# Softmax row sums: addition and reciprocal on GpSimd in place of VectorE

## The chip, the cores and the metric

The kernel runs on one core of a Trainium2 chip. A core has five engines with instruction queues of their own, each working through its queue in order: TensorE (PE, with its weight loads shown as PEld), VectorE (DVE), ScalarE (ACT), GpSimd (POOL) and SyncE (SP), which here issues the DMAs. They work at the same time and wait for one another by semaphores. The metric is the time of one execution on the device in microseconds, the median of several.

## What is computed

Attention with a learned bias of relative position, and after it a soft mixture of experts over the tokens of all eight batches. The part that matters here is the softmax of the attention:

```
scores = scale * q @ k^T + bias
scores = scores - max(scores, axis=-1)
attn = exp(scores)
attn = attn / (sum(attn, axis=-1) + 1e-09)
out  = attn @ v
```

There are 8 batches and 8 heads, 576 positions and a head width of 64, all in 32-bit floats. The mixture of experts then has 32 slots over 512 features, and takes the softmax of its logits once over the tokens and once over the slots. The change touches neither of these two softmaxes, only that of the attention.

## The kernel before

The kernel first builds the table of the bias (some 36 jobs, steps f, B, E, D), stores it in HBM, and reads it back for each pair of heads. Then come 32 units, each a pair of heads of one batch. A unit is cut into row blocks of 128 query positions: four for every unit, and for every second unit a fifth, which holds the last 64 positions of two units. That makes 144 row blocks. Each row block goes through these steps, with p the block and u the unit:

- S (L439, L444): PE multiplies queries and keys, 288 columns at a time, for two heads.
- t (L459): VectorE adds the bias to the scores in PSUM, writes the result to a tile y of 2 x 576 columns in SBUF, and keeps the running minimum (the sign is turned) in mn. Four instructions a block.
- e (L468): ScalarE takes the exponential of 576 columns in place, and puts their sum into one of the two columns of the tile sm. Two instructions a block.
- m (L475, L476): VectorE adds 1e-9 to both columns of sm and takes the reciprocal. This is the step that changes.
- n (L374, called at L483): GpSimd multiplies 576 columns of y by one column of sm, in place. Two instructions a block.
- T and R (L423): PE turns the block through its transposes into PSUM; c and cR (L377): VectorE or ScalarE, as the order says, copies it to the tiles at and ar.
- M and Mr (L547, L557): PE multiplies with the values; x (L377) copies the result to xts.

The last pair of heads adds the steps of the mixture of experts for each batch (L582 to L841), and after the loop come the experts' matrices and the output (L967 to L1075).

The order of all these steps is written out by hand in the string ORDER (L23 on). Each step has one place in it, such as `m0/5` for step m of block 0 in unit 5. The program issues the steps sorted by their place, so every engine gets its own instructions in that order, and none overtakes another on the same engine. The buffers are rotated: four tiles y, four tiles mn and four tiles sm. A tile of sm is written by e, worked on by m and read by n. All DMAs of the loop are issued by SP.

Before the loop, a small tile nb1 (L309) holds the negative of a bias column, one column wide; VectorE reads it at L902 while the table of the bias is built. GpSimd has a few tasks of its own at the start (the identity matrix, zeroing, rsum, the sign of phi at L301), and during the loop only step n and seven small memsets (L690).

Of the kernel before, what the change touches and what calls it, by code (L numbers as in the profile page):

```python
# [10 lines left out]
F32 = mybir.dt.float32  # L11
F32R = mybir.dt.float32r
AF = mybir.ActivationFunctionType
ALU = mybir.AluOpType
# [214 lines left out]
def body(ctx, tc, qk, v, wcol, phi, mw1, mw2, tabh, consth, out, outr):  # L229
    nc = tc.nc  # L230
    P = 128
# [8 lines left out]
    const = ctx.enter_context(tc.tile_pool(name="const", bufs=1))  # L240
# [46 lines left out]
    cols = const.tile([P, 2 + H], F32, name="cols")  # L287
# [18 lines left out]
            nc.gpsimd.memset(t, 0.0)  # L306

    last = {}
    nb1 = const.tile([P, 1], F32, name="nb1")  # L309
    nc.vector.tensor_scalar(out=nb1, in0=cols[:, 1:2], scalar1=-1.0, scalar2=None, op0=ALU.mult)  # L310
    wbd = const.tile([P, 32], F32, name="wbd")
    nc.vector.memset(wbd, 0.0)
    for g in range(4):
        rs = slice(32 * g, 32 * g + 32)
        nc.vector.tensor_scalar(out=wbd[rs, H * g:H * g + H], in0=cols[rs, 2:2 + H], scalar1=1.0 / QS, scalar2=None,
                                op0=ALU.mult)
# [108 lines left out]
    def rows(u, p):  # L425
# [46 lines left out]

        def sums(_):
            r = d["sm", p]
            nc.vector.tensor_scalar(out=r, in0=r, scalar1=1e-9, scalar2=None, op0=ALU.add)  # L475
            nc.vector.reciprocal(out=r, in_=r)  # L476

        step(u, f"m{p}", sums)
        for g in range(2):

# [683 lines left out]
```

## Time and profile before

| | |
|---|---|
| median of three executions | 583.1 us (582.52 to 585.4) |
| span of the profiled execution | 579.5 us (its time as a whole is not shown) |
| VectorE, addition at L475 | 144 instructions, 251 ns in the mean |
| VectorE, reciprocal at L476 | 144 instructions, 166 ns in the mean |
| GpSimd, scaling at L374 | 288 instructions, 746 ns in the mean |
| ScalarE, exponential at L468 | 288 instructions, 770 ns in the mean |

The span runs from the first to the last instruction that the profiler saw; a whole execution is a little longer. In the profile's rows, `y<-y,sm` names the tile that is written and those that are read, `128x2 f32` is partitions by elements, and `x144` is the number of instructions. Busy time comes first, then the mean of one instruction, then the idle time of the engine just before them with what ended it. A wait with several causes is put down to the last one by the profile. "The chain" is the work that ended last, followed back from the last instruction; "the loop" here is the window from 60 to 500 us.

### The profile page before, as it was taken

The numbers are of one execution on the slowest core, as the hardware profiler recorded it, in microseconds if no ns is written. First come the engines' busy times: TensorE is split into PE (matmuls) and PEld (weight loads), VectorE is DVE, ScalarE is ACT, GpSimd is POOL, SyncE is SP. The second block draws the span as 40 slices with busy tenths as digits, with TensorE's granted clock in tenths as the row PEclk, the third lists the DMA queues.
The fourth block names the chain that finished last, engine by engine and source line by source line (L and its number), as shares of the span: only waits on it lengthen the run. The fifth ranks groups of instructions, "written<-read, shape, count | busy, mean of one in ns | idle before, by whom it ended". The sixth has DMA issues, their size and how long they took to land.

```text
span 579.5 us, 19040 instructions
## 1 busy us (share of the span) xinstructions
PE 546.3 (94%) x7235; PEld 351.7 (61%) x7235; DVE 452.6 (78%) x1808; ACT 460.0 (79%) x959; POOL 217.6 (38%) x308
## 2 busy tenths in 40 slices
PE   5989899999999999999999999999999999979992
PEld 3445566666766666666776666676666666643541
DVE  7998878788889788888788888888997889761322
ACT  6989889988888998888988889888879788431332
POOL 4000545555545454454544454545235331400000
PEclk9999899999999999999999999999999999999997
DMA  5698523164865154777522266430533534799968
GB/s 157 225 321 292 167 64 111 56 195 136 293 188 190 51 176 154 255 240 248 170 82 83 85 202 185 148 117 29 184 138 124 173 128 155 260 401 409 403 273 314
DMA packets 43869, 109.89 MB, mean 190 GB/s; under 512 B 8449, under 2 KB 8577, under 8 KB 43777
## 3 DMA queue, kind: packets, MB, share of 16 engines
q1 hardware_dynamic: 43776, 108.67, 54.5%
q8 instruction: 57, 0.93, 0.7%
q14 instruction: 36, 0.29, 0.2%
HBM read 81.25 MB, written 27.41 MB: 188 GB/s over the span
## 4 chain that ended last, share of the span: by engine, by line
PE 64%; DVE 11%; ACT 10%; DMA 6%; issue 4%; POOL 2%; SPq 0%; ACTq 0%; POOLq 0%; DVEq 0%
PE ps L547 16%; PE ps L439 16%; PE ps L423 13%; DVE y L459 6%; ACT y L468 4%; PE ps L444 3%; PE ps L557 3%; PE ps L1030 2%; POOL y L374 2%; PE ps L986 2%; ACT f L900 2%; PE ps L911 2%; ACT e L921 2%; DMA bias_m<-e 1%; DMA xo<-xs 1%
## 5 line engine op out<-in xcount | busy, mean ns | idle before, releaser
L374 POOL TENSOR_SCALAR y<-y,sm 128x576 f32<-128x576 f32 x288 | 210.4, 746 | 274.0 <-DVE sm L476 213.8
L468 ACT ACTIVATE y<-y,mn 128x576 f32<-128x576 f32 x288 | 220.8, 770 | 20.3 <-DVE mn L459 15.5
L439 PE MATMUL ps<-qk 64*128 64x288 f32 x1024 | 160.2, 422 | 1.2 <-DMA qk<-in_qk_dram 0.4
L377 ACT COPY at<-ps 128x1024 f32<-128x1024 f32 (+2 forms) x151 | 132.1, 895 | 23.2 <-PE ps L423 19.3
L547 PE MATMUL ps<-at,v 128*64 128x320 f32 (+1 forms) x1024 | 133.7, 410 | 0.7 <-DMA v<-in_v_dram 0.4
L459 DVE CUSTOM_DVE_ANT_0 y<-ps,bm,mn 128x288 f32<-128x288 f32 x256 | 123.5, 512 | 8.8 <-PE ps L439 3.4
L423 PEld LDWEIGHTS ps<-ident,y 64*128 64x128 f32 x2592 | 100.0, 139 | 43.4 <-POOL y L374 17.8
L459 DVE CUSTOM_DVE_ANT_0 y<-ps,bm 128x288 f32<-128x288 f32 x256 | 108.3, 453 | 15.0 <-PE ps L439 8.7
L423 PE MATMUL ps<-ident,y 64*128 64x64 f32 x2592 | 113.3, 227 | 3.4 <-DVE mn L459 1.0
L439 PEld LDWEIGHTS ps<-qk 64*128 64x128 f32 x1024 | 100.3, 187 | 18.7 <-DVE mn L459 2.8
L547 PEld LDWEIGHTS ps<-at,v 128*64 128x64 f32 x1024 | 70.4, 137 | 54.6 <-DVE mn L459 6.9
L468 ACT ACTIVATION_READ_ACCUMULATOR y<-y,mn 128x1 f32 x288 | 54.9, 191 | 0.0
L475 DVE TENSOR_SCALAR sm<-sm 128x2 f32<-128x2 f32 x144 | 36.1, 251 | 20.4 <-ACT y L468 20.0
L911 PE MATMUL ps<-f,wbd 128*32 128x79 f32 (+45 forms) x640 | 43.4, 407 | 7.0 <-DVE f L902 4.2
L902 DVE TENSOR_SCALAR f<-tabs,scl,nb 128x560 f32<-128x560 f32 (+17 forms) x106 | 45.8, 506 | 2.7 <-DMA tabs<-in_tab_dram 0.9
L459 DVE DVE_READ_ACCUMULATOR2_ANT mn<- 128x1 f32 x576 | 47.6, 83 | 0.0
L911 PEld LDWEIGHTS ps<-f,wbd 128*32 128x32 f32 x640 | 22.8, 114 | 27.9 <-issue 10.1
L377 DVE COPY at<-ps 128x1024 f32<-128x1024 f32 (+2 forms) x41 | 31.2, 763 | 5.5 <-PE ps L423 5.0
L900 ACT ACTIVATE f<-tabs,cols,scl 128x432 f32<-128x432 f32 (+15 forms) x38 | 26.5, 753 | 2.5 <-DMA bias_m<-e 2.5
L476 DVE RECIPROCAL sm<-sm 128x2 f32<-128x2 f32 x144 | 23.8, 166 | 4.9
L921 ACT ACTIVATE e<-ps,bcon 128x591 f32<-128x591 f32 x36 | 25.8, 769 | 0.3 <-PE ps L911 0.3
L444 PE MATMUL ps<-qk 64*64 64x288 f32 x256 | 22.6, 429 | 1.5 <-ACT at L377 1.2
(151 smaller groups left out, 430.5 us busy)
## 6 DMA issues: line engine op xcount, KB each, us to landing
wt<-in_moe_w_dram SPq DMA_DIRECT2D x62, 512.0 KB, 7.1
qk<-in_qk_dram SPq DMA_DIRECT2D x32, 576.0 KB, 4.1
bias_m<-e SPq DMA_DIRECT2D x32, 295.5 KB, 3.4
v<-in_v_dram SPq DMA_DIRECT2D x32, 288.0 KB, 4.4
out_dram<-ob SPq DMA_DIRECT2D x16, 512.0 KB, 5.7
xs<-xts SPq DMA_DIRECT2D x24, 288.0 KB, 3.7
xo<-xs SPq DMA_DIRECT2D x8, 864.0 KB, 4.9
bm<-bias_m SPq DMA_DIRECT2D x16, 288.0 KB, 4.1
```

The lines of the kernel that those rows point to most:

```text
L374: nc.gpsimd.tensor_scalar(out=out, in0=y, scalar1=r, scalar2=1.0, op0=ALU.mult, op1=ALU.mult)
L377: (nc.vector.tensor_copy if eng else nc.scalar.copy)(out=out, in_=in_)
L423: nc.tensor.matmul(out, src[rs], ident[rs, rs], is_transpose=True, start=True, stop=True, tile_position=(64 * r, 0))
L439: nc.tensor.matmul(pss[hh].t[:, 0:HALF], x[rs, S + p * P:S + (p + 1) * P], x[rs, k0:k0 + HALF], start=True, stop=True, tile_position=(64 * ...
L444: nc.tensor.matmul(pss[hh].t[64 * r:64 * r + 64, 0:HALF], x[rs, S + 512:2 * S], x[rs, k0:k0 + HALF], start=True, stop=True, tile_position= ...
L459: nc.vector.tensor_tensor_reduce(out=d["y", p][:, hs], in0=d["ps", p, n][hh].read()[:, 0:HALF], in1=biases[hp][p][:, hs], scale=-QS, scala ...
L468: nc.scalar.activation(out=y, in_=y, func=AF.Exp, bias=d["mn", p][:, 2 + hh:3 + hh], scale=-1.0, accum_out=d["sm", p][:, hh:hh + 1])
L547: nc.tensor.matmul(po.t[o:o + 64, 0:wide[c]], d["v"][:, 64 * (4 * hh + i):64 * (4 * hh + i) + 64], main[:, :, 4 * hh + i, :], start=i == 0 ...
L900: nc.scalar.activation(out=f, in_=tabs[:, 0:n], func=AF.Relu, bias=cols[:, 1:2], scale=sc)
L902: nc.vector.tensor_scalar(out=f, in0=tabs[:, 0:n], scalar1=sc, scalar2=nb1[:, 0:1], op0=ALU.mult, op1=ALU.max)
L911: nc.tensor.matmul(pb.t[32 * t:32 * t + 32, a // 512, a % 512:a % 512 + c1 - c0], wbd, x, start=True, stop=True, tile_position=(0, 32 * t))
L921: nc.scalar.activation(out=e, in_=x, func=AF.Identity, bias=bcon[:, k:k + 1])
```

## The change

Both instructions of step m go to GpSimd. The addition becomes a tensor_scalar with two operations, an addition of 1e-9 and a multiplication by 1. The reciprocal becomes a tensor_tensor that raises sm to the power of a second tile, which holds -1 in both columns. That tile is part of nb1, now four columns wide, and is set by a memset of GpSimd at the start; VectorE writes only the first column of nb1 now. Step m keeps its places in ORDER, and nothing else is changed.

```diff
-    nb1 = const.tile([P, 1], F32, name="nb1")
-    nc.vector.tensor_scalar(out=nb1, in0=cols[:, 1:2], scalar1=-1.0, scalar2=None, op0=ALU.mult)
+    nb1 = const.tile([P, 4], F32, name="nb1")
+    minus = nb1[:, 2:4]
+    nc.gpsimd.memset(minus, -1.0)
+    nc.vector.tensor_scalar(out=nb1[:, 0:1], in0=cols[:, 1:2], scalar1=-1.0, scalar2=None, op0=ALU.mult)
...
         def sums(_):
             r = d["sm", p]
-            nc.vector.tensor_scalar(out=r, in0=r, scalar1=1e-9, scalar2=None, op0=ALU.add)
-            nc.vector.reciprocal(out=r, in_=r)
+            nc.gpsimd.tensor_scalar(out=r, in0=r, scalar1=1e-9, scalar2=1.0, op0=ALU.add, op1=ALU.mult)
+            nc.gpsimd.tensor_tensor(out=r, in0=r, in1=minus, op=ALU.pow)
```

## The prediction

> **What bounds the kernel now.** I read the page's first parts, then the table of engine times for the loop alone, then the chain and the waits. The page gives the frame:
>
> ```profile
> span 579.5 us, 19040 instructions
> ...
> PE 546.3 (94%) x7235; PEld 351.7 (61%) x7235; DVE 452.6 (78%) x1808; ACT 460.0 (79%) x959; POOL 217.6 (38%) x308
> ...
> PE 64%; DVE 11%; ACT 10%; DMA 6%; issue 4%; POOL 2%; SPq 0%; ACTq 0%; POOLq 0%; DVEq 0%
> ```
>
> The edit acts in the attention loop only, about 60 to 500 us. The table of busy times for that window (us busy, instructions in brackets):
>
> ```profile
> core 0: us, PE busy (x) PEld busy (x) DVE busy (x) ACT busy (x) POOL busy (x), PEclk, DMA share, GB/s
> 60.00:500.00 440.00, 432.70 (x5687) 291.36 (x5688) 370.19 (x1596) 383.79 (x826) 209.55 (x293) 1.00 0.46 151
> ```
>
> TensorE is busy 432.7 of 440 us at a granted clock of 1.00, so only 7.3 us are plainly idle there. A busy PE is not quite a full one, though. On the chain, the same eight score products take two lengths (start, us, what):
>
> ```profile
> 69.84 1.24 PE ps L439 x8
> ...
> 79.14 1.02 PE ps L439 x8
> ```
>
> 1.02 us when they run back to back, 1.24 when something is waited for in between. So PE is the bound, with a few us of slack inside it; VectorE (84% of the loop) and ScalarE (87%) are close behind, GpSimd (48%) is not. What can be gained is limited by PE, and what can be lost is not limited at all. The groups the edit touches, in the page's list of costliest groups:
>
> ```profile
> L374 POOL TENSOR_SCALAR y<-y,sm 128x576 f32<-128x576 f32 x288 | 210.4, 746 | 274.0 <-DVE sm L476 213.8
> ...
> L475 DVE TENSOR_SCALAR sm<-sm 128x2 f32<-128x2 f32 x144 | 36.1, 251 | 20.4 <-ACT y L468 20.0
> ...
> L476 DVE RECIPROCAL sm<-sm 128x2 f32<-128x2 f32 x144 | 23.8, 166 | 4.9
> ```
>
> There are 144 row blocks, each with one addition, one reciprocal and two scalings by GpSimd.
>
> **What is removed.** VectorE loses 36.1 + 23.8 = 59.9 us of work, and 20.4 + 4.9 = 25.3 us in which it stood still in front of these two. That is 85 us of its 440. Only the part on the chain can shorten the kernel. In the chain of work, followed through the loop in pieces of 40 us, L475 and L476 stand in 39 rows with 7.1 us together; the first two and the last two are:
>
> ```profile
> 100.95 0.09 DVE sm L475
> 101.06 0.18 DVE sm L476
> ...
> 480.03 0.18 DVE sm L475
> 480.23 0.04 DVE sm L476
> ```
>
> They come in two kinds. Six times, first at 100.95 and last at 444.48 us, the chain goes on from the reciprocal to GpSimd's scaling (0.27 + 0.53 + 0.54 + 0.75 + 0.86 + 0.27 = 3.2 us of the 7.1). The other times, 3.9 us, it goes on to VectorE's next score addition at L459, which merely stood behind them in VectorE's queue. The second kind vanishes.
>
> Part of that time is waiting inside the instruction. The instructions of the two lines, minimum, median and maximum in ns:
>
> ```profile
> L475 DVE TENSOR_SCALAR sm<-sm x144: 147/168/749, 58.1 to 497.7; 128x2 f32<-128x2 f32 x144
> L476 DVE RECIPROCAL sm<-sm x144: 165/166/168, 58.3 to 498.0; 128x2 f32<-128x2 f32 x144
> ```
>
> The addition has a median of 168 and a maximum of 749, about one scaling of GpSimd (746); the reciprocal never varies. So the addition is sometimes held while GpSimd works on SBUF: (251 - 168) x 144 = 12 us, within the 36.1, which goes too.
>
> **What is added.** GpSimd gets 144 additions and 144 powers on 128x2, and one memset at the start (I cost it at nothing: GpSimd stands 7.2 us for the phi load at the start, the first row below, and a 128x1 memset takes 0.1 us, the last row, which is the price without that cover). No row shows a power, nor a 128x2 operation of GpSimd. The nearest, in the list of groups on that engine:
>
> ```profile
> L301 POOL TENSOR_SCALAR phis<-phis 128x256 f32<-128x256 f32 x1 | 3.7, 3737 | 7.2 <-DMA phis<-in_moe_phi_dram 7.2
> ...
> L303 POOL TENSOR_TENSOR rsum<-rsum,ident 128x32 f32<-128x32 f32 x1 | 0.2, 249 | 0.0
> ...
> L1141 POOL MEMSET const-float32-1.0<- 128x1 f32 x1 | 0.1, 98 | 0.0
> ```
>
> Each is bounded below by 0.1 us (the memset) and above by 3.7 us (the dearest single instruction of this engine, though on 256 columns and beside VectorE's run of f additions). For the addition I take 0.25 us, the two-operand row, which has sixteen times the columns. For the power I take 0.25 us too, since two columns can hold little beyond the fixed cost; this is the weakest number here, and its upper end makes the second rival. Together 0.5 us a block, 72 us in all: GpSimd goes from 209.6 to about 281 of 440 us, still the least loaded engine.
>
> On this place the Trainium skill speaks against the change: "GPSIMD Engine Reference", section "Engine selection", sends elementwise work to VectorE and puts GpSimd at about half its speed for two inputs. By it the pair would take about 2 x (251 + 166) = 0.83 us, an estimate, and the gain below would be about 3 us smaller; no row here shows the pair.
>
> **The path of one block.** From the end of the exponential's sum to the scaling, in the timeline at 217 us:
>
> ```profile
> 217.54 0.19 ACT L468 ACTIVATION_READ_ACCUMULATOR y<-y,mn 128x1 f32 x1
> ...
> 217.75 0.17 DVE L475 TENSOR_SCALAR sm<-sm 128x2 f32<-128x2 f32 x1 [0.93 <-ACT y L468]
> 217.96 0.17 DVE L476 RECIPROCAL sm<-sm 128x2 f32<-128x2 f32 x1
> ...
> 218.29 2.90 POOL L374 TENSOR_SCALAR y<-y,sm 128x576 f32<-128x576 f32 x4 [0.90 <-DVE sm L476]
> ```
>
> 217.73 to 218.29: 0.56 us when VectorE was already waiting. After the change: 0.5 us of work and a hop less. So the unobstructed path stays about as long; what goes is VectorE's queue ahead of it.
>
> **The added wait.** GpSimd now waits for the exponential itself. Queued behind it are the block's own two scalings and, by a count in the written ORDER, in 43 of the 144 blocks also scalings of another block, ahead of the block's own; those could pass before, and now stand behind an exponential. PE's turns (T, R) wait for the scalings, and through the four y buffers the later score additions. No DMA is moved: all go by SP, which has neither step.
>
> ```profile
> POOL y L374 <- DVE sm L476: 213.8, 80, 44.3
> ...
> DVE sm L475 <- ACT y L468: 20.0, 33, 1.8
> ...
> PEld ps L423 <- POOL y L374: 17.8, 42, 0.6
> ...
> DVE y L459 <- PE ps L439: 12.1, 21, 1.2
> ```
>
> In this list of waits (us, times, longest) PE's weight loads stood 42 times for a scaling, 0.42 us each, and another view has the matmuls themselves idle for it for 0.8 us in four waits: mostly the wait hides under matmuls that are still running.
>
> ```profile
> PE ps L423 <- POOL y L374: 0.8, 4, 0.3
> ```
>
> **The sum.** On the chain 7.1 us go. Back come 6 x 0.5 = 3.0 us where the chain went through the pair to GpSimd, and at most 4 x 0.5 = 2.0 us for the four visits to GpSimd that had no pair in front. That leaves 2.1 us at the worst, 7.1 at the best. I take 3.6: nearer the low end, because behind each gap PE's own order is late next. Span 579.5 - 3.6 = 575.9. The executions' median is 583.1, 3.6 us above the profiled span (start and end around it; the profiled execution's own total is not shown), so 583.1 - 3.6 = **579.5 us**, its own range 576 to 582.
>
> **Rivals.**
>
> *No gain.* PE is busy for 98% of the loop, so what VectorE leaves turns into VectorE waiting for PE (already 12.1 us at L459, in the list of waits), and the in-order waits on GpSimd eat the rest. About 583, within 2.
>
> For it speaks PE's 432.7 of 440; against it the chain, which leaves PE for VectorE and ScalarE for 21% of the span. Another reason for the same outcome would be that VectorE's remaining work is held by GpSimd's longer activity:
>
> ```profile
> L459 DVE CUSTOM_DVE_ANT_0 y<-ps,bm,mn x256: 495/514/519, 47.6 to 493.0; 128x288 f32<-128x288 f32 x128
> ```
>
> L459 is 495 to 519 ns at every one of 256, with GpSimd busy nearly half the time, so it is never held. The Trainium skill, "Perfetto Trace Analysis", section "Optimizing Scalar/DVE Operations", warns that the two engines share an SBUF port, so that offloading between them might not help. By that warning the time would be 583; this row bears it out for L475 only, the instruction that leaves.
>
> *A dear power: slower.* If the pair takes 1.5 us instead of 0.5, the scalings come 1.5 - 0.56 = 0.94 us later. Where PE waited already, 42 times, some 0.42 us hide as they do now, so 42 x 0.52 = 22 us are lost: about 605. The loss begins near 0.56 + 0.42 = 1.0 us a pair. From (440 - 209.6) / 143 = 1.6 us GpSimd itself is the bound; at 3.7 us for the power alone it would need 144 x (1.49 + 0.25 + 3.7) = 783 us for a loop of 440, a time above 900. Against it: two columns, the 249 ns row. For it: a power is not an addition or a product, and none of this engine's rows does more than these.
>
> *The change doesn't do what it says.* The steps could keep VectorE waiting through another dependence, for instance on the shared tile nb1. VectorE writes nb1 once and waits there for a DMA anyway; nothing follows. It would give 583 and is counted with no gain.
>
> **How the numbers follow.** Forecast (pair up to 0.7 us, gain 1 to 10): 0.48, of which 0.40 beyond 0.5% and 0.08 within. No gain: 0.22, all within 0.5%. Dear power: 0.30, of which 0.28 slower beyond 0.5% and 0.02 within; a third of it, 0.10, lies above 605. About 0.5% (2.9 us) is what a measurement of this kernel tells from no change; the three runs of before span that. So faster 0.40, same 0.32, slower 0.28. The range goes down to 573, where the 7.3 idle us of PE and an estimated 3 us of stretched products are gone, and up to 605, the dear power at 1.5 us; above and below lie about 0.15.
>
> **What would show it.** Right: GpSimd's two new groups at 0.2 to 0.35 us each, its busy time in the loop near 281 us; VectorE near 310 us, with L459 waiting longer for PE; no VectorE row of sm; L374 still near 746 ns. PE's weight loads wait for L374 no more than 18 us. Wrong in price: a power above 0.7 us, GpSimd above 340 us, PE idle for L374 for several us. Wrong in the order: GpSimd idle for exponentials while scalings lie behind, and PE's turns waiting for those.

## The result: slower by 9%, and the profile after

The changed kernel took 635.75 us (632.7 to 641.02), the kernel before 582.81 beside it: ratio 1.0912, 95% interval 1.0855 to 1.097. The forecast was 579.5 with a range of 573 to 605, so the sign was wrong and the time lies outside the range. Ratios compare undisturbed executions alone: one of the nine of the kernel without any pair, below, took 1299.89 us and does not enter its ratio. (Lines of the changed kernel are two higher behind the edit: the pair is L477 and L478, the scaling L376, the score addition L461, the turns L425.)

The page of the changed kernel, span and busy times:

```profile
span 630.9 us, 19013 instructions
...
PE 554.6 (88%) x7235; PEld 345.5 (55%) x7235; DVE 404.7 (64%) x1520; ACT 461.7 (73%) x959; POOL 346.2 (55%) x597
```

VectorE lost 452.6 - 404.7 = 48 us of busy time. The prediction took off 59.9, the two groups' times added up; but their records overlap in time with those of VectorE's neighbouring instructions, and without the pair the busy time of before would be 406.9 us, 46 less. GpSimd gained 346.2 - 217.6 = 129 us instead of 72. The loop now ends near 550 us. The list of groups on GpSimd shows the price of each step:

```profile
L376 POOL TENSOR_SCALAR y<-y,sm 128x576 f32<-128x576 f32 x288 | 210.9, 747 | 8.6
L478 POOL TENSOR_TENSOR sm<-sm,nb 128x2 f32<-128x2 f32 x144 | 100.7, 699 | 12.0
L477 POOL TENSOR_SCALAR sm<-sm 128x2 f32<-128x2 f32 x144 | 27.6, 192 | 177.5 <-ACT y L470 170.4
```

The addition takes 192 ns, the scaling is unchanged, and the power takes 699 ns on two columns. One block in GpSimd's timeline shows the gaps as well (start, us):

```profile
240.06 0.19 POOL L477 TENSOR_SCALAR sm<-sm 128x2 f32<-128x2 f32 x1
240.34 0.70 POOL L478 TENSOR_TENSOR sm<-sm,nb 128x2 f32<-128x2 f32 x1
241.13 1.47 POOL L376 TENSOR_SCALAR y<-y,sm 128x576 f32<-128x576 f32 x2
```

From the start of the addition to the scaling are 1.07 us: 0.89 of work and two gaps of 0.09. The path before was 0.56 us. No wait is printed at 240.06: GpSimd came to this pair late, straight from other scalings. The list of waits (total, times, longest) shows where the time went:

```profile
POOL sm L477 <- ACT y L470: 170.4, 59, 42.9
PEld ps L425 <- POOL y L376: 78.4, 93, 2.4
ACT at L379 <- PE ps L425: 61.0, 66, 2.7
PE ps L425 <- POOL y L376: 48.9, 69, 2.3
```

PE itself now stands idle 69 times for a scaling, 48.9 us, where it was 0.8 us in four. That is nearly the whole loss, 53 us of time and 51 us of the profiled span. Only 59 of the 144 pairs begin with a wait for the exponential; 84 of the others start within 0.1 us of the end of GpSimd's earlier work, so there GpSimd is already behind. ScalarE's copies wait for the late turns in their turn. The chain of work is no use here: its printed shares add up to about half the span, so I don't read it.

### The profile page after: what moved, and what is told of

Read it like the earlier page. It is cut to its first block, busy times and chain, and to the rows that moved or that the text cites. A ratio compares the mean times of both kernels' runs of the same rounds, so it can differ in the third digit from the quotient of the medians.

```text
span 630.9 us, 19013 instructions
## 1 busy us (share of the span) xinstructions
PE 554.6 (88%) x7235; PEld 345.5 (55%) x7235; DVE 404.7 (64%) x1520; ACT 461.7 (73%) x959; POOL 346.2 (55%) x597
## 4 chain that ended last, share of the span: by engine, by line
PE 20%; POOL 17%; ACT 6%; DVE 4%; issue 3%; DMA 1%; POOLq 0%; DVEq 0%; SPq 0%; ACTq 0%
POOL y L376 11%; POOL sm L478 5%; PE ps L425 4%; ACT y L470 4%; PE ps L441 3%; PE ps L1032 2%; PE ps L988 2%; DVE y L461 2%; PE ps L549 2%; DMA xo<-xs 1%; POOL sm L477 1%; PE ps L1065 1%; ACT at L379 1%; PE ps L765 1%; DVE ob L379 1%
## 5 line engine op out<-in xcount | busy, mean ns | idle before, releaser
L376 POOL TENSOR_SCALAR y<-y,sm 128x576 f32<-128x576 f32 x288 | 210.9, 747 | 8.6
L425 PE MATMUL ps<-ident,y 64*128 64x64 f32 x2592 | 118.5, 229 | 50.4 <-POOL y L376 48.9
L441 PE MATMUL ps<-qk 64*128 64x288 f32 x1024 | 157.3, 425 | 0.4 <-DVE ck L741 0.3
L425 PEld LDWEIGHTS ps<-ident,y 64*128 64x128 f32 x2592 | 98.5, 140 | 102.6 <-POOL y L376 78.4
L461 DVE CUSTOM_DVE_ANT_0 y<-ps,bm 128x288 f32<-128x288 f32 x256 | 108.2, 454 | 42.4 <-PE ps L441 26.3
L461 DVE CUSTOM_DVE_ANT_0 y<-ps,bm,mn 128x288 f32<-128x288 f32 x256 | 123.1, 514 | 16.4 <-PE ps L441 8.2
L477 POOL TENSOR_SCALAR sm<-sm 128x2 f32<-128x2 f32 x144 | 27.6, 192 | 177.5 <-ACT y L470 170.4
L478 POOL TENSOR_TENSOR sm<-sm,nb 128x2 f32<-128x2 f32 x144 | 100.7, 699 | 12.0
L441 PEld LDWEIGHTS ps<-qk 64*128 64x128 f32 x1024 | 94.4, 190 | 20.7 <-DVE mn L461 3.0
L461 DVE DVE_READ_ACCUMULATOR2_ANT mn<- 128x1 f32 x576 | 47.8, 83 | 0.0
L379 DVE COPY ar<-ps 128x256 f32<-128x256 f32 x22 | 9.3, 424 | 33.9 <-PE ps L425 33.8
L379 DVE COPY xts<-ps 128x320 f32<-128x320 f32 (+1 forms) x26 | 11.4, 455 | 26.8 <-PE ps L559 25.3
```

What stands on the lines that cost most here:

```text
L376: nc.gpsimd.tensor_scalar(out=out, in0=y, scalar1=r, scalar2=1.0, op0=ALU.mult, op1=ALU.mult)
L379: (nc.vector.tensor_copy if eng else nc.scalar.copy)(out=out, in_=in_)
L425: nc.tensor.matmul(out, src[rs], ident[rs, rs], is_transpose=True, start=True, stop=True, tile_position=(64 * r, 0))
L441: nc.tensor.matmul(pss[hh].t[:, 0:HALF], x[rs, S + p * P:S + (p + 1) * P], x[rs, k0:k0 + HALF], start=True, stop=True, tile_position=(64 * ...
L461: nc.vector.tensor_tensor_reduce(out=d["y", p][:, hs], in0=d["ps", p, n][hh].read()[:, 0:HALF], in1=biases[hp][p][:, hs], scale=-QS, scala ...
L477: nc.gpsimd.tensor_scalar(out=r, in0=r, scalar1=1e-9, scalar2=1.0, op0=ALU.add, op1=ALU.mult)
```

## The experiments

Two theories. **Price**: the pair's length on GpSimd makes the scalings late, and PE waits for them. **Order**: GpSimd's place in the order is at fault, since ready scalings stand behind its wait for another block's exponential.

### Length of the pair

A product in place of the power:

```diff
-    nc.gpsimd.memset(minus, -1.0)
+    nc.gpsimd.memset(minus, 0.001)
...
-            nc.gpsimd.tensor_tensor(out=r, in0=r, in1=minus, op=ALU.pow)
+            nc.gpsimd.tensor_tensor(out=r, in0=r, in1=minus, op=ALU.mult)
```

> The power becomes a product with a constant 0.001, in the same place; the reciprocal is left out, so the attention is scaled wrongly, and only the time counts. Price theory (the long power, 0.70 us, makes the scalings late): the pair shrinks from 1.07 us to about 0.55 us per block, as long as VectorE's pair was, and the time goes back to 578 to 590. Order theory (GpSimd waits in its queue for an exponential, and ready scalings of other blocks stand behind it): the waits stay, 610 to 636.

Measured 589.36 us, ratio 1.0117 (1.008 to 1.0155). Its group and PE's wait:

```profile
L478 POOL TENSOR_TENSOR sm<-sm,nb 128x2 f32<-128x2 f32 x144 | 28.1, 195 | 12.0
```

```profile
PE ps L425 <- POOL y L376: 11.9, 27, 1.2
```

A product has 195 ns where the power has 699, the pair is 0.56 us, and most of the loss is gone. So the power's half microsecond is the main cause. But the 0.56 us on GpSimd are not free either.

Three additions in place of one:

```diff
             nc.gpsimd.tensor_scalar(out=r, in0=r, scalar1=1e-9, scalar2=1.0, op0=ALU.add, op1=ALU.mult)
+            nc.gpsimd.tensor_scalar(out=r, in0=r, scalar1=1e-9, scalar2=1.0, op0=ALU.add, op1=ALU.mult)
+            nc.gpsimd.tensor_scalar(out=r, in0=r, scalar1=1e-9, scalar2=1.0, op0=ALU.add, op1=ALU.mult)
             nc.gpsimd.tensor_tensor(out=r, in0=r, in1=minus, op=ALU.pow)
```

> The changed kernel with the addition made three times, two more instructions of 0.19 us with their gaps, 0.55 us more per block. Price theory: as much again as the power's 0.5 us cost, 680 to 700 (144 x 0.37 us more). Order theory: the waits for the exponential are no longer, 636 to 650.

Measured 710.22 us, 1.2198 (1.2142 to 1.2255), above even the price theory's range. PE's idle time for the scalings:

```profile
PE ps L425 <- POOL y L376: 96.9, 87, 3.9
```

The power alone:

```diff
-            nc.gpsimd.tensor_scalar(out=r, in0=r, scalar1=1e-9, scalar2=1.0, op0=ALU.add, op1=ALU.mult)
             nc.gpsimd.tensor_tensor(out=r, in0=r, in1=minus, op=ALU.pow)
```

> The changed kernel without the addition of 1e-9 (left out): the power alone, 0.70 us and a gap, 0.79 us per block in place of 1.07. Price theory: between the runs with a pair of 0.55 us (589.4) and of 1.07 us (635.8), by the line through them 605 to 616. If the power's presence counted, and not the length: 630 to 636.

Measured 600.13 us, 1.0254 (1.02 to 1.0309), below the straight line. Taking 0.28 us from the pair gives back 36 us.

And the zero of the curve, no pair on any engine:

```diff
-            nc.vector.tensor_scalar(out=r, in0=r, scalar1=1e-9, scalar2=None, op0=ALU.add)
-            nc.vector.reciprocal(out=r, in_=r)
+            pass
```

> The kernel before with neither addition nor reciprocal on any engine (both left out; the scaling multiplies by the sum itself, so the attention is not normalised). The whole of VectorE's relief, with nothing given back: the zero of the curve of the pair's length. By the forecast's chain at most 7.1 us go, so 576 or more. If the relief is worth more than the chain shows, as the run without the addition (576.3 with half of it) suggests: 566 to 574.

Measured 578.44 us, 0.9918 (0.9885 to 0.9951), a gain of 4.8 us: within the 7.1 of the forecast's chain, and not the 566 to 574 of the other reading.

| pair on GpSimd, start to scaling | time | ratio to before | PE idle for the scalings |
|---|---|---|---|
| none | 578.4 us | 0.992 | none listed |
| 0.56 us (product) | 589.4 | 1.012 | 11.9 us, 27 times |
| 0.79 (power alone) | 600.1 | 1.025 | 19.2, 37 |
| 1.07 (the change) | 635.8 | 1.091 | 48.9, 69 |
| 1.63 (three additions) | 710.2 | 1.220 | 96.9, 87 |

The slope is 20 us of time for a microsecond of pair up to 0.56, then 47, and 127 to 133 beyond 0.79. The runs come from different sets; by the ratios the steps are 21, 35, and 134 to 137. With 144 blocks, the last figure means that about 0.9 of every microsecond added to a block arrives at the end. Not all of that is waiting. With the longest pair the granted clock of the profiled execution is 0.942, where the changed kernel has 0.987; a score product (L441) takes 460 ns instead of 425, and PE is busy 29 us longer. PE's idle time for the scalings grew by 48 of the 73 us by which the span grew. Why the clock was lower is open.

### Place in the order

The pair directly ahead of the block's own first scaling (`done` is an empty set at the start):

```diff
-        step(u, f"m{p}", sums)
...
             def scale(_, g=g):
+                if (u, p) not in done:
+                    done.add((u, p))
+                    sums(0)
                 y = d["y", p][:, S * g:S * g + S]
```

> The changed kernel with the pair moved in GpSimd's queue to directly ahead of the block's own first scaling, so that no other block's scaling stands behind its wait. Order theory: most of the 53 us come back, 583 to 600. Price theory: pair and price are as before, 620 to 640.

Measured 633.17 us, 1.087 (1.0817 to 1.0922), against 635.75. The same edit on the product version:

> The product version (589.4) with the pair moved directly ahead of the block's own first scaling; the reciprocal is left out. Order theory for what was left there: 581 to 585. Price theory (0.55 us of occupation for each block): 587 to 592.

Measured 586.08 us, 1.0046 (1.0028 to 1.0064), against 589.36, between the two ranges. Both moves give back about 3 us, the first within the intervals, the second just beyond them. The order theory is worth that and no more.

The wait by itself was tried twice. The first form reads the sums on GpSimd ahead of VectorE's pair (`spare` is a further part of nb1, kept for no use):

```diff
+            nc.gpsimd.tensor_scalar(out=spare, in0=r, scalar1=1e-9, scalar2=1.0, op0=ALU.add, op1=ALU.mult)
             nc.vector.tensor_scalar(out=r, in0=r, scalar1=1e-9, scalar2=None, op0=ALU.add)
             nc.vector.reciprocal(out=r, in_=r)
```

> The kernel before, with VectorE's pair as it was, and on GpSimd, in the place of the pair, one addition of 0.19 us that reads the sums and writes a spare tile: the wait in GpSimd's queue without the price. Order theory: most of the 6.7 us that the product version still lost, 588 to 595. Price theory: 583 to 587, 0.28 us of occupation.

Measured 608.74 us, 1.0398 (1.0335 to 1.0462): too much for either theory. The list of waits names a wait that I had built in myself:

```profile
DVE sm L479 <- POOL nb L478: 70.3, 84, 2.3
```

VectorE works on sm in place, so it may not begin before GpSimd has read it, and stood 70.3 us for that. The clean form lets VectorE write two columns of mn that are free by then:

```diff
+            nc.gpsimd.tensor_scalar(out=spare, in0=r, scalar1=1e-9, scalar2=1.0, op0=ALU.add, op1=ALU.mult)
-            nc.vector.tensor_scalar(out=r, in0=r, scalar1=1e-9, scalar2=None, op0=ALU.add)
-            nc.vector.reciprocal(out=r, in_=r)
+            nc.vector.tensor_scalar(out=d["mn", p][:, 0:2], in0=r, scalar1=1e-9, scalar2=None, op0=ALU.add)
+            nc.vector.reciprocal(out=d["mn", p][:, 0:2], in_=d["mn", p][:, 0:2])
...
-                norm(y, y, d["sm", p][:, g:g + 1])
+                norm(y, y, d["mn", p][:, g:g + 1])
```

> The kernel before, VectorE's pair writing its result to two spare columns of mn, and on GpSimd in the pair's place one addition of 0.19 us that reads the sums and writes a spare tile. As the run with the wait alone (608.7), but VectorE no longer waits for GpSimd to have read the sums. If that wait of VectorE made the 608.7: 584 to 592. If GpSimd's own wait in its queue did: 600 to 610.

Measured 590.87 us, 1.0127 (1.0098 to 1.0155). Its control has the same addition on constants, behind the block's second scaling:

```diff
-            nc.gpsimd.tensor_scalar(out=spare, in0=r, scalar1=1e-9, scalar2=1.0, op0=ALU.add, op1=ALU.mult)
...
                 norm(y, y, d["mn", p][:, g:g + 1])
+                if (u, p) in done:
+                    nc.gpsimd.tensor_scalar(out=spare, in0=minus, scalar1=1e-9, scalar2=1.0, op0=ALU.add, op1=ALU.mult)
+                done.add((u, p))
```

> The same kernel with GpSimd's addition on constants behind the block's second scaling, with no wait: its occupation alone. Price theory: 583 to 590 and within 3 us of the run with the clean wait. Order theory: that run is at least 8 us slower than this one.

Measured 588.88 us, 1.0102 (1.007 to 1.0134). The wait is worth 2 us, within the intervals nothing. But 0.19 us of GpSimd per block, which nobody waits for, already cost 6 us. PE's idle time for the scalings is 5.3 us in that run, where it was 0.8 before. Both runs also write VectorE's result to mn, and that was not timed by itself.

### The path, or GpSimd's occupation

One power per block behind the second scaling, nothing in the path:

```diff
                 norm(y, y, d["sm", p][:, g:g + 1])
+                if (u, p) in done:
+                    nc.gpsimd.tensor_tensor(out=spare, in0=minus, in1=minus, op=ALU.pow)
+                done.add((u, p))
```

> The kernel before, with VectorE's pair as it was, and one power per block on a spare tile, on GpSimd behind the block's second scaling: GpSimd's extra occupation without a longer path in the block itself and without a wait. If occupation is what costs: 600 to 620. If only the path from exponential to scaling costs, or the order: 583 to 588.

Measured 600.6 us, 1.0299 (1.0256 to 1.0342). Occupation alone costs 18 us, and nearly as much appears as PE's idle time for the scalings:

```profile
PE ps L427 <- POOL y L378: 15.5, 27, 1.4
```

The same instruction in the path, behind VectorE's pair, with `minus` set to 1:

```diff
             nc.vector.reciprocal(out=r, in_=r)
+            nc.gpsimd.tensor_tensor(out=r, in0=r, in1=minus, op=ALU.pow)
```

> The kernel before, with VectorE's pair as it was, and behind it in the same place a power of plus one on GpSimd (the value unchanged), so that the scalings wait for it. The same instruction as in the run with powers behind the scalings (600.6), now in the path: 0.56 + 0.78 = 1.34 us from exponential to scaling. If the path counts: 655 to 685, by the line through pairs of 1.07 and 1.62 us. If only GpSimd's occupation counts: 597 to 605.

Measured 639.45 us, 1.0918 (1.085 to 1.0986). That is 39 us more for the same occupation (36 by the ratios), less than the line through the longer pairs gave: my path of 1.34 us predicted 655 or more. Path and occupation both count.

Last, half of the scalings to VectorE, in the changed kernel and in the one before:

```diff
-                norm(y, y, d["sm", p][:, g:g + 1])
+                if g:
+                    nc.vector.tensor_scalar(out=y, in0=y, scalar1=d["sm", p][:, g:g + 1], scalar2=None, op0=ALU.mult)
+                else:
+                    norm(y, y, d["sm", p][:, g:g + 1])
```

> The changed kernel with the second scaling of each block on VectorE (in the same places of the order), which has been relieved of the pair. The path from exponential to the first scaling stays 1.07 us; GpSimd's work per block falls from 2.54 to about 1.8 us. If GpSimd falls behind in its queue: 585 to 605. If the path alone costs: 620 to 640.

> The control: the kernel before with the second scaling of each block on VectorE. VectorE gets some 65 us more and may be held while GpSimd scales; GpSimd has half its work. If VectorE's load counts little: 580 to 590; if it counts as much as its relief did (6 us for 36 us): 590 to 600.

Measured 620.33 us, 1.0647 (1.0601 to 1.0693), and for the control 617.34, 1.0593 (1.0539 to 1.0648). Neither is where I looked for it, because the control loses 34 us of its own. Between the two, however, the pair on GpSimd makes no clear difference: 3 us, where it makes 53 with all scalings on GpSimd. In the changed kernel with the half moved, the waits read:

```profile
POOL sm L477 <- ACT y L470: 238.2, 82, 43.6
...
DVE y L486 <- POOL sm L478: 37.6, 45, 2.0
...
PE ps L425 <- DVE y L486: 6.5, 13, 0.8
...
PE ps L425 <- POOL y L376: 3.6, 7, 0.8
```

GpSimd now waits at 82 pairs instead of 59, and PE's idle time for it falls from 48.9 to 3.6 us, though the pair is as long as before. Part of the waiting has moved: PE stands 6.5 us for VectorE's scaling (L486), and VectorE 37.6 us for the power. Even so PE's idle time for scalings of either engine is 10 us and not 49. That speaks for GpSimd falling behind when pairs and scalings of several blocks meet in its queue. It is not a proof: this kernel has another brake on VectorE, which may cover what the pair costs.

### What VectorE's relief is worth, and a faster kernel

The reciprocal alone on VectorE:

```diff
-            nc.vector.tensor_scalar(out=r, in0=r, scalar1=1e-9, scalar2=None, op0=ALU.add)
             nc.vector.reciprocal(out=r, in_=r)
```

> The kernel before without the addition of 1e-9 (left out), the reciprocal alone on VectorE. It takes 36 us of busy time and part of the 25 us of standing still from VectorE, with nothing given back: what relief of VectorE is worth. If the chain's 7.1 us are worth what I forecast: 577 to 581. If PE's own work bounds the kernel whatever VectorE does: 582 to 584.

Measured 576.32 us, 0.9852 (0.9801 to 0.9902): faster than both kernels, and a little below the 577 to 581 expected. The sum holds the exponential of the row's maximum, which is 1, and 1e-9 added to 1 or more changes nothing in 32 bits. Its page and group:

```profile
span 574.8 us, 18836 instructions
...
PE 545.0 (95%) x7235; PEld 353.0 (61%) x7235; DVE 417.6 (73%) x1664; ACT 459.9 (80%) x959; POOL 218.0 (38%) x308
...
L475 DVE RECIPROCAL sm<-sm 128x2 f32<-128x2 f32 x144 | 22.7, 161 | 29.3 <-ACT y L468 28.2
```

The instruction that left is the one that could be held by GpSimd; the reciprocal that stayed is not (168 ns at the most). The trace of before shows the holding: 41 of the 144 additions took more than 200 ns, and each of them met a running scaling of GpSimd and ended within 0.12 us after the end of one.

## Why the prediction was wrong, point by point

**What bounds the kernel: right.** PE is the bound before, and the loss shows as PE's own idle time.

**What is removed: right.** Without the pair on any engine the gain is 2.9 to 6.7 us by its interval; the forecast had 7.1 us at the most before anything was given back. Without the addition alone the interval reaches from 5.7 to 11.6 us. Why taking half away gave no less than taking all is open; both runs lie 2.1 us from each other, in different sets.

**What is added: wrong, and this step failed first.** I took 0.25 us for the power, since "two columns can hold little beyond the fixed cost". It takes 0.70 us in the mean, and 688 ns at the least:

```profile
L478 POOL TENSOR_TENSOR sm<-sm,nb x144: 688/700/734, 58.0 to 550.8; 128x2 f32<-128x2 f32 x144
```

A product of the same shape takes 195 ns, so 0.50 us belong to the operation itself. The row that I rested on was an addition; no row of the trace bore on a power. In the experiments this half microsecond is worth 46 of the 53 us (635.8 against 589.4). The addition was right (0.25 taken, 0.19 measured), and the two gaps of 0.09 were not counted.

The rule that I weighed there, the Trainium skill's "GPSIMD Engine Reference", section "Engine selection" (VectorE for elementwise work, GpSimd at about half its speed for two inputs and roughly at line rate for one), had the sign right. My estimate from it, 0.83 us, doubled the addition as well, which has only one input, and took VectorE's 251 ns with the time in which it was held. Measured are 1.07 us with the gaps. For the power against VectorE's reciprocal the ratio is 699 / 166 = 4.2, for the additions 192 against 168 in the median.

**The path of one block: wrong by the price.** It grew from 0.56 to 1.07 us.

**The added wait: right that it would matter little.** 2 to 3 us in each pair of runs that moved it, in two of the three within the intervals.

**The sum: wrong even at the price that I took.** It charged the pair only at the ten places where the chain of before passed through GpSimd, 5.0 us at the most. The run with the product has a pair of about the forecast's size (0.39 us of work, 0.56 with the gaps). It took 589.4 us, where the kernel without any pair took 578.4: 11 us were given back, and PE's idle time for the scalings is 11.9 us there. So a power as cheap as a product would still have ended 1.2% above the kernel before, and not below it.

**The rival of the dear power: right mechanism, its size far off.** Its formula kept the 42 waits of before and let 0.42 us of each hide, so that loss began at 1.0 us a pair and reached 22 us at 1.5. For the measured pair it gives 42 x (1.07 - 0.98) = 4 us; measured are 53. Both terms were wrong. The 0.42 us that a weight load stands for a scaling are no spare time of the block: the pair of 0.56 us loses already, far below 0.98. And the number of waits is not fixed: weight loads waiting for a scaling rise from 42 to 57, 72, 93 and 109 over the five kernels from the one before to the longest pair. A later scaling turns blocks that never waited into blocks that do. GpSimd's mean load hid this. With powers behind the scalings it was busy for 294.54 of 440 us in the same window, 67% in place of 48%, and 18 us were already gone (busy us of PE, PEld, DVE, ACT and POOL):

```profile
60.00:500.00 440.00, 420.24 (x5413) 276.71 (x5413) 355.86 (x1536) 371.55 (x794) 294.54 (x421) 0.99 0.44 145
```

**The range** took its upper end from that formula, at a pair of 1.5 us, and so failed though the pair itself lay inside it.

**VectorE's other work held by GpSimd: rightly ruled out.** L461 still has 505 to 520 ns with GpSimd busier.

## What to carry to other kernels

Where the trace has no row of an operation, a row of another operation of the same shape bounds only the fixed cost; measure the operation itself before moving it onto a path. An engine that is half idle in the mean is not free when its work comes in bursts: what counts is how often its queue is already behind when the work arrives, and a delay there must be charged to every block that it could make late, not to those that wait now. If a term is exactly absorbed in the rounding, leave it out before looking for an engine to carry it.

## What the hardware showed that I had not expected

A scaling on VectorE and one on GpSimd hold each other. In the changed kernel with half of the scalings moved (minimum, median, maximum in ns):

```profile
L477 POOL TENSOR_SCALAR sm<-sm x144: 191/193/521, 58.7 to 538.5; 128x2 f32<-128x2 f32 x144
L478 POOL TENSOR_TENSOR sm<-sm,nb x144: 688/701/998, 59.0 to 538.9; 128x2 f32<-128x2 f32 x144
L486 DVE TENSOR_SCALAR y<-y,sm x144: 499/520/1052, 59.8 to 539.6; 128x576 f32<-128x576 f32 x144
L376 POOL TENSOR_SCALAR y<-y,sm x144: 739/752/1075, 59.8 to 539.7; 128x576 f32<-128x576 f32 x144
```

GpSimd's addition, which never left 191 to 194 ns in the changed kernel, reaches 521, its median and 328 ns more. VectorE's scaling reaches 1052, twice its median. The Trainium skill, "SBUF — State Buffer", section "SBUF: two separate sides", describes a port pair for which GpSimd competes with VectorE's operations in a two-port mode or with two inputs from SBUF; the one that starts first holds it for its whole instruction. The rows agree with that in both directions. The score addition, which reads one of its two tensors from PSUM, is spared (498 to 520 ns in this run). Whether the held operations of VectorE ran in such a mode, and why the reciprocal is not held, no run here shows.
